# Weight pieces of four heads from each half of the heads, instead of eight heads in a row

## The chip, the cores and the metric

The kernel runs on one core of a Trainium2 chip. The time is device microseconds for one launch, from runs without the profiler. Three runs of the kernel before gave 1760.65, 1762.07 and 1762.35 us. Differences under 0.2% (3.5 us) can hardly be told from no change here.

## The reference, cut to what matters

Two blocks share an input of 2048 rows of 640 values. Block A is an attention whose memory is handed from segment to segment: 64 segments of 32 rows run one after the other, each with 8 memory rows that are the first 8 output rows of the segment before. Block B is a feed-forward block with a gate. The output mixes the two per row. All tensors are bfloat16.

```python
for s in range(n_seg):                      # 64 segments, in order
    xs = x[:, s*32:(s+1)*32, :]
    h = jnp.concatenate([mem, xs], axis=1)  # 8 + 32 rows
    q = jnp.einsum('btd,dhe->bhte', h, Wq)  # 32 heads of 192, Wq is 640 x 32 x 192
    k = jnp.einsum('btd,dhe->bhte', h, Wk)
    v = jnp.einsum('btd,dhe->bhte', h, Wv)
    p = softmax(mask(q k^T * 192**-0.5))
    o = jnp.einsum('bhte,hed->btd', p v, Wo)   # sum over all 32 heads
    mem = o[:, :8, :]                       # the next segment waits for this
    outs.append(o[:, 8:, :])
b = (gelu(x @ w_gate) * (x @ w_up)) @ w_down
return g * concat(outs) + (1 - g) * b       # g = sigmoid(sum(x * gate_w))
```

The heads don't meet before the sum in Wo, so it is free which heads are worked on together, as long as the rows of Wo match.

## The kernel before, in words

**Order of the whole.** Block B goes first (four blocks of 512 rows, up to about 160 us) while the weights of A are loaded. Then come the 64 segments, some 24.5 us each.

**Pieces of weights.** Wq, Wk and Wv are cut into 20 pieces each: piece `(m, o, k)` holds, for one group `o` of 8 heads (4 groups, 1536 columns) and one of 5 slices `k` of the model dimension, 128 partitions of 1536 values, 384 KB. Partition p of slice k is row 5p + k of the matrix, so that in HBM the rows of a piece stand 61,440 bytes apart, and each is one run of 3072 bytes (`piece_src`, L491 to L495). Wo is cut into 16 pieces `(3, p)`, one for each pair of heads, each one solid block of 480 KB, 3840 bytes to a partition.

**Swapped slots.** All 76 pieces don't fit into SBUF. 13 slots of Q, K and V pieces (3 Wq, 5 Wk, 5 Wv) are shared by head group 0 and head group 3, and 3 slots of Wo by pairs 0 to 2 and pairs 13 to 15 (`partner`, L545 to L549). Even segments go through the groups as 0, 1, 2, 3, odd ones as 3, 2, 1, 0. So in every segment the group that comes first is in place, each of its 13 + 3 slots is loaded anew as soon as TensorE has read it, and the new pieces are needed by the last group of the same segment; the next segment begins with that group. `swap_loads` (L612) puts these loads into the program behind the item that read the slot, and `load_piece` (L597) issues them, all on SyncE's queue (SP).

**Order within a segment.** The list `PROG` (L506) is the order of the work for TensorE: projections ("g", L1046 and, where the stationary operand is kept, L226), scores (L1087 to L1100), transposed probabilities (L1144, L1149), probabilities times V (L1177, L1179), the products with Wo of the first three groups (L1206), and those of the last group (L1229) as the segment's last work. `proj` takes the Q, K and V pieces by `piece`, `wo_part` those of Wo. VectorE then adds up the segment's output and transposes the 8 memory rows (L1371, L1375), and the next segment's first projection waits for that. Projections of the memory rows' outputs of other segments ("lf", L884) are spread over the list.

**Other work on SP's queue.** Between the weight loads SP issues, in program order, stores of pre-computed Q and K columns into a scratch (L895, L1276) and their loads (L935), the output stores (L956), the loads of x (L706) and of block B's result (L947). SP waits at each issue until the buffer is free, and the loads behind it in the queue wait with it. TensorE waits for a piece at the first matmul that reads it.

**At the start.** Before the segments, 40 pieces of Wq and Wk are issued in one row between 23 and 59 us (`load_residents`, L636, and `load_tmp`, L631), just ahead of the x load for the third block of B (L675).

Of the kernel before, what the change touches and what calls it, by code (L numbers as in the profile page):

```python
# [231 lines left out]
def _build(nc, A_x, A_mem0, A_Wq, A_Wk, A_Wv, A_Wo, seg_len, w_gate, w_up, w_down,  # L232
# [12 lines left out]
    NPAIR = NT // 2  # L245
    NOCT = NT // 4
# [13 lines left out]
    OW = 4 * 384  # L260
# [6 lines left out]
    S_ = _Sched(nc)  # L267
# [65 lines left out]
    o = wsA_base - wsB_total  # L333
# [6 lines left out]
    o = wsA_base  # L340
# [4 lines left out]
    o = ffn_base  # L345
# [4 lines left out]
    def bview(o, nbytes, plo=0, phi=128):  # L350
        return arena[plo:phi, o // 2:(o + nbytes) // 2]
# [4 lines left out]
    def sreg(o, nbytes, plo=0, phi=128):  # L356
        return Rg("sb", o, o + nbytes, plo, phi)
# [74 lines left out]
    o = ffn_base - sum(fp_sz.values())  # L432
# [50 lines left out]
    def psb(bank):  # L483
        return ps[:, bank, :].bitcast(BF)

    Wq2 = A_Wq.rearrange("d h e -> d (h e)").rearrange("(p k) n -> p k n", p=128)
    Wk2 = A_Wk.rearrange("d h e -> d (h e)").rearrange("(p k) n -> p k n", p=128)
    Wv2 = A_Wv.rearrange("d h e -> d (h e)").rearrange("(p k) n -> p k n", p=128)
    Wo2 = A_Wo.rearrange("h e n -> (h e) n").rearrange("(t p c) n -> p t c n", p=128, c=3)

    def piece_src(key):  # L491
        if key[0] == 3:
            return Wo2[:, key[1]]
        m, o_, k = key
        return (Wq2, Wk2, Wv2)[m][:, k, OW * o_:OW * (o_ + 1)]  # L495

    def piece_size(key):
        return GO if key[0] == 3 else GQ

    def piece_view(key, o):  # L500
        if key[0] == 3:
            return bview(o, GO).rearrange("p (c n) -> p c n", n=Dm)
        return bview(o, GQ)
# [16 lines left out]
    assert NOCT == 4  # L520
    WOP = 4
    NWP = NT
    NSW = 3
    NSQ = 13
    assert NWP == WOP * NOCT and 2 * NSW <= NWP

# [3 lines left out]
    def wo_pairs(s, item):  # L530
        lo, n = (WOP * item[1], WOP) if len(item) == 2 else (WOP * item[1] + 2 * item[2], 2)
        return [p if s % 2 == 0 else NWP - 1 - p for p in range(lo, lo + n)]
# [27 lines left out]
    tmp_off = {key: len(lk) * GQ + i * GQ for i, key in enumerate(lt)}  # L560
    assert (len(lk) + len(lt)) * GQ <= fp_base
    seq = lk + lv[2] + lw[NLW:] + lv[0] + lv[1] + lw[:NLW]
    res_off = {}
    o = 0
# [7 lines left out]
    r_res = {key: sreg(o, piece_size(key)) for key, o in res_off.items()}  # L572
# [23 lines left out]

    def load_piece(key, name):  # L597
        loaded[slot_id[key]] = key
        S_.add("sp", lambda e: e.dma_start(piece_view(key, res_off[key]), piece_src(key)), writes=[r_res[key]],
               dma_sem="slot%d" % slot_id[key], name="%s %s" % (name, key))  # L600

    def piece(seg, key):
# [9 lines left out]
    def swap_loads(seg, item):  # L612
        if item[0] == "g" and item[1] == 0 and 0 < item[2] < KT - 1:
            later.extend(key for key in done_keys if key[0] == 1)
            done_keys[:] = [key for key in done_keys if key[0] != 1]
        elif later:
            done_keys[:] = sorted(done_keys + later, key=lambda key: key[:1] + key[2:])
            del later[:]
        for key in done_keys:
            other = swap_in.get(key)  # L620
            if other is None or (other in partner) == (seg % 2 == 0):
                continue
            load_piece(other, "swap s%d" % seg)
        del done_keys[:]
# [5 lines left out]

    def load_tmp():  # L631
        for key in tmp_off:
            S_.add("sp", lambda e, key=key: e.dma_start(piece_view(key, tmp_off[key]), piece_src(key)),
                   writes=[r_tmp[key]], dma_sem="tmp%d" % (KT * key[0] + key[2]), name="tmp %s" % (key,))

    def load_residents(cls, pick=lambda key: True):  # L636
        for key in first:
            if slot_class[key] == cls and pick(key):
                load_piece(partner[key] if key in tmp_off else key, "res")
# [39 lines left out]
    for h in range(NH):  # L679
        for w_, sb_, rw_, nm in ((w_gate, wg_sb, r_wg, "wg"), (w_up, wu_sb, r_wu, "wu")):  # L680
            S_.add("sp", lambda e, h=h, w_=w_, sb_=sb_: e.dma_start(
                sb_[h], w_.rearrange("(p k) f -> p k f", p=128)[:, :, FH * h:FH * (h + 1)]),
                writes=[rw_[h]], dma_sem="%s%d" % (nm, h))
# [154 lines left out]
    x_stage(0)  # L838
    load_residents(0)
    load_tmp()  # L840
    for blk in range(NFB):
        if blk:
# [578 lines left out]
def bass_gated_mix__memory_aug_recurrent_mem_tr__glu_gated_geglu__prompt_kernel(  # L1421
    nc,
    A_x,
    A_mem0,
    A_Wq,
    A_Wk,
    A_Wv,
    A_Wo,
    A_seg_len,
    B_x,  # L1430
    B_w_gate,
    B_w_up,
    B_w_down,
    gate_w,
    out,
):
    _build(nc, A_x, A_mem0, A_Wq, A_Wk, A_Wv, A_Wo, A_seg_len, B_w_gate, B_w_up, B_w_down, gate_w, out)
# [33 lines left out]
```

## Time and profile before

| | |
|---|---|
| median of three runs | 1762.07 us (1760.65 to 1762.35) |
| span of the profiled execution | 1765.1 us |
| TensorE matmuls busy | 1623.9 us, 92% of the span |
| VectorE, ScalarE, GpSimd busy | 960.0, 802.8, 320.0 us |
| granted TensorE clock, mean | 0.994 |
| moved by DMA | 499.57 MB, mean 283 GB/s |
| share of the 16 DMA engines' time, SP's queue | 78.3% |
| weight loads in the profile | 335 Wk, 335 Wv, 209 Wq of 384 KB; 205 Wo of 480 KB |

In the profile PE is TensorE's matmuls, PEld its weight loads, DVE VectorE, ACT ScalarE, POOL GpSimd, SP SyncE; an engine's name with a q is its queue of waits and DMA issues. L599 is line 599 of the kernel. A group's "idle before" is the idle time of its engine ahead of it. A DMA's time "to landing" runs from its issue to the semaphore that tells of its last byte. The profiled execution is 3.0 us (0.17%) longer than the median without the profiler.

### The profile page before, as it was taken

Reading aid. Unit: us, or ns where it says so; the run is one execution under the profiler, and the core shown is the slowest. Engines: PE = TensorE matmul, PEld = TensorE weight load, DVE = VectorE, ACT = ScalarE, POOL = GpSimd, SP = SyncE. Lnnn points to the kernel's source line nnn. Section 1 sums busy time; section 2 is a strip of 40 time slices with the busy share of each in tenths; the row PEclk is TensorE's granted clock in tenths of the full one; section 3 lists DMA queues with packets and bytes.
Section 4 is the critical chain, followed back from the end, with each engine's and each line's share of the span. In section 5 each row is a group of like instructions: output and inputs, shape, how many; then the busy total and the mean of one; then the engine's idle time right before and its main releaser. Section 6 shows DMA issues by size and latency. Waiting matters only on the chain.

```text
span 1765.1 us, 80301 instructions
## 1 busy us (share of the span) xinstructions
PE 1623.9 (92%) x39162; PEld 809.5 (46%) x31501; DVE 960.0 (54%) x2932; ACT 802.8 (45%) x1835; POOL 320.0 (18%) x1099
## 2 busy tenths in 40 slices
PE   9999999999999999999999989999999998999887
PEld 4554444444444444454444444454444444454444
DVE  2222655556555655555555655555555655655554
ACT  3222544545444544444444544444444544445443
POOL 1100111111112112111212111111211121121211
PEclk9999999999999999999999999999999999999999
DMA  9814987888778887888788887879787886879776
GB/s 335 295 48 157 329 313 250 320 313 288 280 269 311 299 308 253 315 290 319 281 280 293 296 293 250 314 285 323 279 280 275 311 310 241 312 282 327 283 275 238
DMA packets 271311, 499.57 MB, mean 283 GB/s; under 512 B 105304, under 2 KB 132208, under 8 KB 270960
## 3 DMA queue, kind: packets, MB, share of 16 engines
q1 hardware_dynamic: 267832, 491.34, 78.3%
q8 instruction: 276, 4.52, 1.0%
q10 hardware_dynamic: 3128, 3.09, 0.6%
q14 instruction: 75, 0.61, 0.1%
HBM read 473.22 MB, written 21.11 MB: 280 GB/s over the span
## 4 chain that ended last, share of the span: by engine, by line
PE 71%; DVE 15%; DMA 6%; issue 4%; ACT 4%; DVEq 0%; SPq 0%; ACTq 0%
PE ps L1046 20%; PE ps L226 15%; PE ps L1206 8%; DMA arena<-in_A_Wo_dram 5%; PE ps L1177 3%; PE ps L804 3%; PE ps L801 3%; PE ps L884 3%; PE ps L1100 3%; PE ps L819 2%; PE ps L1087 2%; DVE ps L1114 2%; DVE arena L1112 2%; PE ps L1095 2%; PE ps L1229 2%
## 5 line engine op out<-in xcount | busy, mean ns | idle before, releaser
L1046 PE MATMUL ps<-arena 128*32 128x384 bf16 x9940 | 723.0, 329 | 42.4 <-DVE arena L1375 34.4
L226 PE MATMUL ps<-arena 128*32 128x384 bf16 x7680 | 595.4, 328 | 7.9 <-DVE arena L1215 3.5
L1046 PEld LDWEIGHTS ps<-arena 128*32 128x32 bf16 x9940 | 257.5, 97 | 365.3 <-issue 226.0
L1080 DVE STREAM_TRANSPOSE arena<-arena 128x384 bf16<-128x384 bf16 x512 | 270.8, 557 | 150.8 <-ACT arena L1066 149.2
L1066 ACT ACTIVATE arena<-ps 128x384 bf16<-128x384 f32 x512 | 236.2, 489 | 211.6 <-PE ps L1046 196.3
L1206 PE MATMUL ps<-arena 128*32 128x320 bf16 x6144 | 293.6, 301 | 13.9 <-issue 13.4
L1124 ACT ACTIVATE ps<-ps 104x160 f32<-104x160 f32 x256 | 71.9, 281 | 293.4 <-DVE ps L1114 293.4
L1206 PEld LDWEIGHTS ps<-arena 128*32 128x32 bf16 x6144 | 163.5, 97 | 74.0 <-issue 19.4
L1112 DVE TENSOR_REDUCE arena<-ps 104x4 f32<-104x160 f32 x256 | 83.0, 324 | 165.8 <-PE ps L1100 164.6
L941 POOL COPY arena<-arena 128x96 bf16<-128x96 bf16 x256 | 70.3, 275 | 513.4 <-PE ps L1100 444.2
L1188 ACT ACTIVATE arena<-ps 128x480 bf16<-128x480 f32 (+1 forms) x256 | 137.0, 535 | 43.8 <-PE ps L1179 39.6
L1196 POOL COPY arena<-arena 128x96 bf16<-128x96 bf16 x256 | 68.3, 267 | 441.1 <-ACT arena L1188 357.3
L1162 ACT ACTIVATE arena<-ps 128x448 bf16<-128x448 f32 x192 | 104.2, 543 | 96.7 <-PE ps L1149 96.4
L1069 ACT ACTIVATE arena<-ps 128x384 bf16<-128x384 f32 x256 | 125.1, 489 | 20.9 <-PE ps L1046 16.3
L1177 PE MATMUL ps<-arena 128*64 128x160 bf16 x1536 | 123.1, 243 | 12.5 <-ACT arena L1162 6.9
L1126 DVE TENSOR_REDUCE arena<-ps 104x4 f32<-104x160 f32 x256 | 83.0, 324 | 92.5 <-ACT ps L1124 92.5
L1177 PEld LDWEIGHTS ps<-arena 128*64 128x64 bf16 x1536 | 80.8, 109 | 91.6 <-issue 31.7
L884 PE MATMUL ps<-arena 128*32 128x384 bf16 x1280 | 111.4, 330 | 2.2 <-issue 2.0
L1179 PE MATMUL ps<-arena 128*64 128x64 bf16 x1536 | 104.8, 193 | 4.1 <-issue 4.1
L891 DVE STREAM_TRANSPOSE arena<-arena 128x384 bf16<-128x384 bf16 x128 | 73.7, 576 | 31.6 <-ACT arena L889 27.8
L1215 DVE TENSOR_TENSOR arena<-ps,arena 64x160 f32<-64x160 f32 x160 | 50.8, 317 | 72.3 <-ACT arena L1212 61.6
L1114 DVE TENSOR_TENSOR ps<-ps,arena 104x160 f32<-104x160 f32 x256 | 85.0, 332 | 8.8
(84 smaller groups left out, 1819.2 us busy)
## 6 DMA issues: line engine op xcount, KB each, us to landing
arena<-in_A_Wk_dram SPq DMA_DIRECT2D x335, 384.0 KB, 7.1
arena<-in_A_Wv_dram SPq DMA_DIRECT2D x335, 384.0 KB, 9.1
arena<-in_A_Wo_dram SPq DMA_DIRECT2D x205, 480.0 KB, 6.4
arena<-in_A_Wq_dram SPq DMA_DIRECT2D x209, 384.0 KB, 5.4
arena<-left_qk_scratch SPq DMA_DIRECT2D x126, 96.0 KB, 2.8
left_qk_scratch<-arena SPq DMA_DIRECT2D x49, 192.0 KB, 2.3
left_qk_scratch<-arena SPq DMA_DIRECT2D x30, 96.0 KB, 5.7
ffn_b_scratch<-arena ACTq DMA_DIRECT2D x16, 160.0 KB, 4.4
```

What stands on the lines that cost most here:

```text
L226: return e.add_instruction(mybir.InstMatmult(name=nm, start_tensor_calc=like["start"], stop_tensor_calc=stop, tile_size=(128, 32), tile_po ...
L884: fns.append(lambda e, outp=outp, rhs=rhs, j=j: e.matmul(outp, lhs, rhs, start=(k == 0), stop=(k == KT - 1), tile_position=(0, 32 * j)))
L1046: fns.append(lambda e, outp=outp, rhs=rhs, j=j: e.matmul(outp, lhs, rhs, start=(k == 0), stop=(k == KT - 1), tile_position=(0, 32 * j)))
L1066: S_.add("act", lambda e, m=m, bk=bk: e.activation(out=rows_sb[m], in_=ps[:, bk, 0:384], func=ACTF.Copy), reads=[r_ps[bk]], writes=[r_rows ...
L1069: S_.add("act", lambda e, i=i, bk=bk: e.activation(out=v_sb[i % NVB].rearrange("p (c n) -> p c n", c=3), in_=ps[:, bk, 0:384].rearrange("p ...
L1080: S_.add("dve", lambda e: e.transpose(out=dst[:, :, 0:L], in_=rows_sb[m].rearrange("p (c r) -> p c r", r=L)), reads=[r_rows[m]], writes=[r ...
L1112: S_.add("dve", lambda e: e.tensor_reduce(out=mxs, in_=S3, axis=AX.X, op=ALU.max), reads=[rb], writes=[rst], name="smax max")
L1114: S_.add("dve", lambda e: e.tensor_tensor(out=S3, in0=S3, in1=mxb, op=ALU.subtract), reads=[rb, rst], writes=[rb], name="smax sub")
L1177: return [lambda e: e.matmul(full, v[:, e0:e0 + 64], PTm[:, i], start=True, stop=False, tile_position=(0, 64 * i), skip_group_check=True), ...
L1179: lambda e: e.matmul(part, vl[:, e0:e0 + 64], PTl[:, i], start=False, stop=True, tile_position=(0, 64 * i), skip_group_check=True)]
L1188: S_.add("act", lambda e: e.activation(out=apx(u[:, 0, 0, :], [[R, na], [3 * R, 4], [1, R]]), in_=ps[:, A, 0:na * W].rearrange("p (c t r) ...
L1206: fns.append(lambda e, i=i, t=t, j=j, gv=gv: e.matmul(ps[32 * j:32 * j + 32, bank, 0:2 * DJ].rearrange("p (h n) -> p h n", h=2), lhs2[i], ...
```

## The change

A head group is no longer 8 heads in a row but 4 heads of the first sixteen and the 4 that stand at the same place among the second sixteen. A row of a Q, K or V piece is then two runs of 1536 bytes, 6144 bytes apart in HBM, where it was one run of 3072 bytes. Both runs go into the same place in SBUF, next to each other, in the same transfer. The pair of heads t of group o is pair 8 (t // 2) + 2 o + t % 2 of the matrix, and the Wo pieces are taken by that; each is still one solid block. The instructions of all engines, their order and the sizes of the tiles are the same; only the addresses from which SP's weight loads read are others.

```diff
+    WOP = 4
...
     def piece_src(key):
         if key[0] == 3:
-            return Wo2[:, key[1]]
+            o_, t = key[1] // WOP, key[1] % WOP
+            return Wo2[:, NPAIR * (t // 2) + 2 * o_ + t % 2]
         m, o_, k = key
-        return (Wq2, Wk2, Wv2)[m][:, k, OW * o_:OW * (o_ + 1)]
+        return (Wq2, Wk2, Wv2)[m][:, k].rearrange("p (h o n) -> p o h n", h=2, o=NOCT)[:, o_]
+
+    def piece_dst(key, o):
+        v = piece_view(key, o)
+        return v if key[0] == 3 else v.rearrange("p (h n) -> p h n", h=2)
...
-        S_.add("sp", lambda e: e.dma_start(piece_view(key, res_off[key]), piece_src(key)), writes=[r_res[key]],
+        S_.add("sp", lambda e: e.dma_start(piece_dst(key, res_off[key]), piece_src(key)), writes=[r_res[key]],
...
-            S_.add("sp", lambda e, key=key: e.dma_start(piece_view(key, tmp_off[key]), piece_src(key)),
+            S_.add("sp", lambda e, key=key: e.dma_start(piece_dst(key, tmp_off[key]), piece_src(key)),
```

More of the change, by code (lines that the diff above doesn't have):

```diff
@@ L520, in _build @@
     assert NOCT == 4
-    WOP = 4
     NWP = NT
```

## The prediction, made before the result was known

> **What bounds the kernel now.** I read the page first, then who waited for the weight loads, then one segment's issues and its chain, and last the speed of the DMA engines with rows of different lengths.
>
> The page:
>
> ```profile
> span 1765.1 us, 80301 instructions
> ...
> DMA packets 271311, 499.57 MB, mean 283 GB/s; under 512 B 105304, under 2 KB 132208, under 8 KB 270960
> ...
> q1 hardware_dynamic: 267832, 491.34, 78.3%
> ...
> PE 71%; DVE 15%; DMA 6%; issue 4%; ACT 4%; DVEq 0%; SPq 0%; ACTq 0%
> ```
>
> TensorE carries 71% of the chain that ended last, but 6% of it, some 106 us, goes through DMAs, and the page's list by line puts 5% on the loads of Wo. Queue q1, SP's, keeps the 16 DMA engines busy for 78.3% of the span. So the DMA engines are the second resource, and not far from the first. Of the packets, 270,960 - 132,208 = 138,752 lie between 2 and 8 KB: they are the 879 Q, K and V loads and the 205 Wo loads, at 128 rows each. A row is one packet.
>
> Who waited for the loads of L599, the weight loads in the segments (us in total, times):
>
> ```profile
>   PEld ps L1229: 8.6, 12
>   PE ps L1229: 6.1, 10
>   PEld ps L1046: 2.4, 6
> ```
>
> With 0.5 us on a fourth row this is 17.6 us in all: TensorE waits little for weights, and nearly always at L1229, the segment's last products with Wo.
>
> One segment (number 5), SP's issues by start and length:
>
> ```profile
> 305.12 0.50 SPq L599 DMA_DIRECT2D arena<-in_A_Wk_dram  x1
> 305.67 2.56 SPq L599 DMA_DIRECT2D arena<-in_A_Wq_dram  x3
> 308.27 2.80 SPq L599 DMA_DIRECT2D arena<-in_A_Wk_dram  x4
> 311.12 2.15 SPq L599 DMA_DIRECT2D arena<-in_A_Wv_dram  x4
> ...
> 314.48 1.58 SPq L599 DMA_DIRECT2D arena<-in_A_Wv_dram  x1
> 318.23 0.38 SPq L1276 DMA_DIRECT2D left_qk_scratch<-arena  x1
> 318.65 1.03 SPq L599 DMA_DIRECT2D arena<-in_A_Wo_dram  x2
> ...
> 320.20 0.55 SPq L599 DMA_DIRECT2D arena<-in_A_Wo_dram  x1
> ```
>
> and its end in the chain:
>
> ```profile
> 320.14 0.06 PE ps L1206
> 320.20 6.85 DMA arena<-in_A_Wo_dram
> 327.05 0.04 issue
> 327.10 0.42 PE ps L1229 x12
> ```
>
> 13 pieces go out within 11 us, and the engines take about 1.0 us for each, so a line forms: the last Wo piece stands 6.85 us in it, lands at 327.05, and the segment's last matmuls start 0.05 us later. What the 13 pieces ahead of it take longer, it lands later.
>
> The same for all segments: I set the landing of each of the 16 swapped pieces against the first matmul that waits for it, from the trace's issues, times to landing and matmuls, and took the smallest spare time of each of the 64 segments. It is at the end of the wait (0.04 us) in 21 segments, 0.1 to 0.6 us in 7, 0.6 to 1 us in 11, 1 to 2 us in 18 and more in 7. Of the segments whose number leaves 1 when divided by 4, which run the most extra work on SP, 15 of 16 have none to spare.
>
> The speed of the DMA engines when they are full: three stretches, 9 to 13 us (w_gate and w_up, 768 bytes a row), 17 to 20 us (w_down, 1280 bytes) and 314 to 319 us (the Q, K and V pieces, 3072 bytes):
>
> ```profile
> DMA packets 1969, 1.48 MB, mean 369 GB/s; under 512 B 48, under 2 KB 1969, under 8 KB 1969
> ...
> DMA packets 941, 1.19 MB, mean 396 GB/s; under 512 B 13, under 2 KB 941, under 8 KB 941
> ...
> DMA packets 737, 2.03 MB, mean 406 GB/s; under 512 B 81, under 2 KB 81, under 8 KB 736
> ```
>
> The reader sees that short rows cost speed, but not much. The rows under 512 B here are the 4-byte semaphore writes.
>
> **The change part by part.** (1) *Engines.* PE, DVE, ACT and POOL get the same instructions in the same order; cost 0, no cover needed. Wo: other blocks, equally solid, 3840 bytes a row; 0.
>
> (2) *Rows.* Each of the 879 Q, K and V loads becomes 256 rows of 1536 bytes instead of 128 of 3072: 112,512 packets more. What does one more packet cost? One engine spends 16 x 768 / 369 = 33.3 ns on 768 bytes, 16 x 1280 / 396 = 51.7 ns on 1280 and 16 x 3072 / 406 = 121.1 ns on 3072. The two short rows give 18.4 ns for 512 bytes and so 5.7 ns that come with any packet. From a line between 1280 and 3072 bytes, 1536 would take 61.6 ns, and two of them 2.1 ns more than one of 3072. The packets' own recorded times (median 36 ns for 768 bytes, 55 for 1280, 121 for 3072), which overlap a little, give 8 ns. So 2.1 to 8 ns, and I take 5.5, since 1536 lies next to the pair of short rows. An engine has 8 rows of each piece: 8 x 5.5 = 44 ns a piece (17 to 64), and 13 pieces put the Wo loads 0.57 us back (0.22 to 0.83).
>
> (3) *What of it TensorE feels.* In each segment I let the nth piece of Q, K or V land n x 44 ns later, Wo 13 x 44 ns, and took the largest amount by which a piece then misses its first matmul. 28 of 64 segments are late, by 12.5 us in sum: 8.6 us in the segments of remainder 1 (15 x 0.57), 2.8 in those of remainder 2, 1.1 in the rest. The next segment starts that much later, with its loads, so the delays add. At 17 ns a piece the sum is 4.4 us, at 33 ns 8.9, at 64 ns 20.5, at 80 ns 27.5. The remaining 36 segments hide the added 0.57 us behind their spare time; without that the sum would be 64 x 0.57 = 36 us.
>
> (4) *SP's issue.* An issue of a piece takes 0.43 us in the median; one of w_gate with 640 rows 0.62 to 0.92 us, a scratch store of 512 rows 0.38. So 0 to 0.2 us more for 256 rows; I take 0, because at 1.0 us a piece the engines stay behind SP either way. At the start SP is held once about 12 pieces are under way; if that limit counts rows, it will be 6. Then the last Wv issue (it lands at 322.73) ends near 317 instead of 316.06. Behind it stands the store that waits for DVE until 318.2; cover 1 us, and if it were gone, the line at the engines would still be 5 us long. The out store and the x load between the Wv loads are in the same line now. Cost 0.
>
> (5) *Who else waits in the line.* SP waits at L935 for a scratch store (72.5 us, 15 times) and at L947 for an output store (25.8 us, 26 times), and GpSimd's L973 and VectorE's L975 need L947's data. All land later by the same 0.57 us, and mostly in segments of remainder 1, where TensorE shifts as much; VectorE has 0.1 to 0.8 us to spare there before the next L1080. Between 0 and 0.57 us in 16 segments, 0 to 9 us; I take 0, since both sides shift together.
>
> (6) *The start.* The x load issued at 58.80 stands behind 40 pieces: 40 x 44 ns = 1.8 us. It lands at 72.39 and its transposes start at 75.27; hidden. At 80 ns it would cost 0.3 us.
>
> Sum: 1765.1 + 12.5 = 1777.6 us in the profile; the median lies 3.0 us under the profile, so 1774 us (+0.7%).
>
> **The rivals.** *No difference.* If the DMA engines move 1536-byte rows as fast as 3072-byte ones, the price per packet falls to the 2.1 ns or to nothing, and the sum to 4 us or less: 1762 to 1765.5. For it: 396 against 406 GB/s are 2.5% apart, and the longer stretch is disturbed by more semaphore writes. Against it: 369 GB/s at 768 bytes. The Trainium skill's page "DMA: Bandwidth & Descriptors" says under Specifications that transfers of 512 bytes and up run at line rate, the rule that speaks for this rival. The trace agrees only in part: 768 bytes reached 91% of the speed of 3072.
>
> *Faster.* The 3072-byte rows took 121 ns in the median but 132 in the mean; some 2,400 of them, 38 a segment, took over 300 ns, mostly as a stream starts. If two runs from places 6144 bytes apart do away with these, a row costs 11 - 5.5, about 6 ns, less, 0.6 us over 13 pieces. In the 21 segments that wait, about 0.5 us of it counts, since some waits are shorter: 10 us, 1752; with all waits gone 17.6 us, 1744. It decides once the saving passes 5.5 ns a row. Against it: 9 of 10 rows already are at the median, and the address pitch between rows is unchanged.
>
> *Much slower.* If such long packets come with each packet rather than with each byte, a row costs 11 + 5.5 = 17 ns more, 0.135 us a piece, 1.8 us at Wo. The sum of step 3 then lies between 36.6 us (0.1 us a piece) and 68.5 (0.155), about 56: 1818. Against it: 768-byte rows were 41 ns in the mean against 36, 1280-byte rows 58.5 against 55; the excess shrinks with the row.
>
> **How the numbers follow.** My forecast (4.5 to 28 us more, 1766.5 to 1790) has 0.66, no difference 0.15, faster 0.08, much slower 0.11. The bound of what can be told from no change is 0.2%, 3.5 us. Slower: 0.66 + 0.11, less 0.01 for a forecast that ends just inside the bound, 0.76; the same 0.16; faster 0.08. The range leaves out the faster case, most of the much slower one and the lower part of no difference: 1762 to 1795.
>
> **What the profile after would show.** Packets of SP's queue up by 112,512 to about 380,000, nearly all of the new ones under 2 KB. The stretch of full engines in a segment at 385 to 400 GB/s instead of 406. Waits at L1229 for the Wo loads up from 14.7 us to about 27, the L1046 waits by 1 or 2 us; DMA's share of the chain up from 6% to 10% or more; busy times of the engines unchanged. It is wrong if the packets don't double, if the speed at 1536 bytes leaves the 369 to 406 GB/s, if the waits grow at lines other than L1229 and L1046, or if SP is held where the Wo loads are issued.

## The result, and the profile after

The changed kernel takes 1791.32 us (median of four runs, 1784.64 to 1794.64), the kernel before beside it 1762.21 us: a ratio of 1.0172, 95% interval 1.0145 to 1.0199. The change costs 29 us, where 12 were forecast. The profiled executions are 25.4 us apart, 1790.5 against 1765.1 us, at granted clocks of 0.997 and 0.994, so the clock is not the cause.

The page of the kernel after (the fourth and fifth lines are DMA queues: packets, MB, share of 16 engines' time):

```profile
span 1790.5 us, 80301 instructions
PE 1627.9 (91%) x39162; PEld 810.0 (45%) x31501; DVE 962.0 (54%) x2932; ACT 802.3 (45%) x1835; POOL 320.3 (18%) x1099
DMA packets 383823, 499.57 MB, mean 279 GB/s; under 512 B 105304, under 2 KB 357232, under 8 KB 383472
q1 hardware_dynamic: 380344, 491.34, 80.5%
q8 instruction: 276, 4.52, 1.0%
PE 69%; DVE 14%; DMA 8%; issue 5%; ACT 4%; DVEq 0%; POOL 0%; ACTq 0%; SPq 0%; POOLq 0%
```

The packets have risen by exactly 112,512, all under 2 KB, and the instructions are the same. In the chain that ended last DMA went from 6% to 8%, and "issue", which the prediction did not look at, from 4% to 5%.

Who waited for the weight loads, now at L604 (the lines after it have moved by 5: L1234 was L1229, L1051 was L1046):

```profile
  PEld ps L1234: 13.8, 19
  PE ps L1234: 10.0, 18
  PEld ps L1051: 7.4, 16
  PE ps L1051: 2.0, 5
```

PEld and PE can stand in the same wait, the weight load into the array and the matmul behind it, so the rows must not be added up, as the prediction did with its 17.6 us. The matmuls alone waited 6.6 us in 12 places before and 12.0 us in 23 after. That is 5 us of the 25.

The rest is in rows that name no releaser. The view of waits, TensorE alone (line, what ended the wait: us in total, times, longest us), of the kernel before:

```profile
PE ps L1206 <- issue: 13.4, 14, 2.0
...
PE ps L1046 <- issue: 5.4, 8, 1.3
PE ps L1177 <- issue: 4.8, 6, 1.5
...
PE ps L1095 <- issue: 0.9, 2, 0.5
...
PE ps L1100 <- issue: 0.8, 2, 0.5
```

and of the kernel after:

```profile
PE ps L1211 <- issue: 14.7, 14, 1.8
...
PE ps L1051 <- issue: 9.7, 13, 1.6
...
PE ps L1182 <- issue: 6.2, 6, 1.5
PE ps L1105 <- issue: 4.5, 8, 1.4
...
PE ps L1100 <- issue: 4.2, 6, 1.0
```

All rows of this kind come to 33.9 us in 48 places before and 51.1 us in 71 after. I laid the idle stretches of matmuls and weight loads together, each stretch counted once: 132.9 us before and 153.9 us after, 21.1 us more (without the 1.4 us at the very start). Of that +17.1 us are "issue", +5.4 us waits for weights, -1.4 us all else. Outside idle stretches TensorE takes 4.2 us longer. Sum 25.3 of the 25.4 us.

What is TensorE waiting for, when no semaphore is late? The same instruction in both kernels, in the timeline of TensorE (start us, length, line, operation, count, idle before and its end). Before:

```profile
393.06 0.26 PE L1095 MATMUL ps<-arena 128*40 128x40 bf16 x7
393.73 0.20 PE L1095 MATMUL ps<-arena 128*40 128x40 bf16 x1 [0.41 <-issue]
```

After:

```profile
398.16 0.26 PE L1100 MATMUL ps<-arena 128*40 128x40 bf16 x7
399.35 0.20 PE L1100 MATMUL ps<-arena 128*40 128x40 bf16 x1 [0.93 <-issue]
```

Eight equal matmuls stand in the program in a row, with no wait between the seventh and the eighth, and yet the eighth starts late, in both kernels. About 2.5 us earlier a packet of another queue was under way; the DMA view of 391.2 to 391.4 us before,

```profile
q8 instruction: 1, 0.02, 33.7%
```

and of 396.6 to 396.8 us after:

```profile
q8 instruction: 1, 0.02, 34.9%
```

The trace gives their starts as 391.32 and 396.68 us, with 1.08 and 1.12 us for each. There are 276 such packets of 16,384 bytes in both kernels. PE and PEld together are 39,162 + 31,501 = 70,663 instructions, and 70,663 / 276 = 256.03. So one packet goes with every 256 instructions of TensorE, and I read it as TensorE's own code. All 44 idle stretches over 0.2 us without a releaser before, and all 66 after, end 2.2 to 2.7 us after the start of such a packet; a moment taken at random does so in about 8% of cases. I read the stretches as TensorE running out of code, because its next 256 instructions came late. That they came late because the packet stood in line with the weight loads is what the experiments have to show. The Trainium skill's page "Runtime: NRT & Kernel Launch" says under Instruction fetch mechanics that code is fetched in blocks of 16 KiB, 256 instructions, and that a crossing is "mostly hidden". The block agrees with the 256.03 here. The cover does not: 34 us are open before and 51 after.

### The profile page after: what moved, and what is told of

Same layout as the page of the kernel before. It is cut to its first block, busy times and chain, and to the rows that moved or that the text cites. A ratio compares the mean times of both kernels' runs of the same rounds, so it can differ in the third digit from the quotient of the medians.

```text
span 1790.5 us, 80301 instructions
## 1 busy us (share of the span) xinstructions
PE 1627.9 (91%) x39162; PEld 810.0 (45%) x31501; DVE 962.0 (54%) x2932; ACT 802.3 (45%) x1835; POOL 320.3 (18%) x1099
## 4 chain that ended last, share of the span: by engine, by line
PE 69%; DVE 14%; DMA 8%; issue 5%; ACT 4%; DVEq 0%; POOL 0%; ACTq 0%; SPq 0%; POOLq 0%
PE ps L1051 19%; PE ps L226 14%; PE ps L1211 7%; DMA arena<-in_A_Wo_dram 7%; PE ps L1182 3%; PE ps L809 3%; PE ps L806 3%; PE ps L1105 3%; PE ps L889 3%; PE ps L824 2%; DVE ps L1119 2%; PE ps L1092 2%; PE ps L1234 2%; DVE arena L1117 2%; PE ps L1100 2%
## 5 line engine op out<-in xcount | busy, mean ns | idle before, releaser
L1051 PE MATMUL ps<-arena 128*32 128x384 bf16 x9940 | 725.4, 329 | 48.1 <-DVE arena L1380 33.8
L1051 PEld LDWEIGHTS ps<-arena 128*32 128x32 bf16 x9940 | 258.5, 97 | 373.3 <-issue 229.5
L1211 PE MATMUL ps<-arena 128*32 128x320 bf16 x6144 | 294.0, 300 | 15.6 <-issue 14.7
L1182 PE MATMUL ps<-arena 128*64 128x160 bf16 x1536 | 123.6, 243 | 13.9 <-ACT arena L1167 6.2
L1234 PE MATMUL ps<-arena 128*32 128x160 bf16 x3072 | 75.0, 234 | 16.8 <-DMA arena<-in_A_Wo_dram 10.0
```

Of the source, the lines that this page charges most:

```text
L1051: fns.append(lambda e, outp=outp, rhs=rhs, j=j: e.matmul(outp, lhs, rhs, start=(k == 0), stop=(k == KT - 1), tile_position=(0, 32 * j)))
L1182: return [lambda e: e.matmul(full, v[:, e0:e0 + 64], PTm[:, i], start=True, stop=False, tile_position=(0, 64 * i), skip_group_check=True), ...
L1211: fns.append(lambda e, i=i, t=t, j=j, gv=gv: e.matmul(ps[32 * j:32 * j + 32, bank, 0:2 * DJ].rearrange("p (h n) -> p h n", h=2), lhs2[i], ...
L1234: S_.add("pe", [lambda e, j=j, c=c, g_=g_, p=p: e.matmul(ps[32 * j:32 * j + 32, OB2, SC:512], u[:, p % 4, c, 0:L], g_[:, c, DJ * j:DJ * (j ...
```

## The experiments

Three theories went into the runs. **A**, the prediction's mechanism with a larger price: rows take longer, the weights land later, TensorE waits for them. **B**: the code packets stand longer behind the weight loads, and TensorE waits for code. **C**: it is the 6144 bytes between the two runs, not their number. For each run I give the matmuls' idle time that ends in "issue" as *code* and the time that ends in a weight load as *weights*, summed from the view of waits. Before: code 33.9, weights 6.6; after: 51.1 and 12.0. Each ratio is to runs of the kernel before taken beside the run (medians 1759.8 to 1768.6 us).

**Runs 3072 bytes apart** (C). The group takes its two runs from one half of the columns:

```diff
-            return Wo2[:, NPAIR * (t // 2) + 2 * o_ + t % 2]
+            return Wo2[:, NPAIR * (o_ // 2) + 2 * (o_ % 2) + 4 * (t // 2) + t % 2]
-        return (Wq2, Wk2, Wv2)[m][:, k].rearrange("p (h o n) -> p o h n", h=2, o=NOCT)[:, o_]
+        half = (Wq2, Wk2, Wv2)[m][:, k, 2 * OW * (o_ // 2):2 * OW * (o_ // 2 + 1)]
+        return half.rearrange("p (h o n) -> p o h n", h=2, o=2)[:, o_ % 2]
```

> Two runs of 1536 bytes to a row as in the changed kernel, but 3072 bytes apart in HBM instead of 6144 (a group is four heads and the four that stand eight heads further on; the Wo pairs match). Theory A (each packet more costs its DMA engine a fixed time, so the weights land later and TensorE waits for them): as the changed kernel, ratio to before 1.013 to 1.021, median row 65 ns. Theory B (TensorE's own code comes over the same engines and comes later): the same ratio. Theory C (it is the place of the two runs in HBM that costs): another ratio, under 1.01 or over 1.03.

1793.97 us, ratio 1.0195 (1.0174 to 1.0217); code 53.3. It is like the changed kernel, so halving the distance changes nothing that can be told, and C falls.

**The order of Wo alone**, Q, K and V as before:

```diff
-            return Wo2[:, key[1]]
+            o_, t = key[1] // 4, key[1] % 4
+            return Wo2[:, NPAIR * (t // 2) + 2 * o_ + t % 2]
         m, o_, k = key
         return (Wq2, Wk2, Wv2)[m][:, k, OW * o_:OW * (o_ + 1)]
```

> The changed kernel's order of the Wo pieces alone, with the rows of Q, K and V of the kernel before (so each head's result meets another head's Wo rows). All theories: no difference, ratio 0.998 to 1.002. If it is over 1.005, the blocks of Wo are part of the cause.

1762.04 us, 1.0019 (1.0002 to 1.0036); code 34.3, weights 7.1. The other Wo blocks cost 0.2%, 0.36% at the most; nearly all of the cost is in the rows of Q, K and V.

**Four runs of 768 bytes**, three packets more to a row instead of one:

```diff
-            return Wo2[:, NPAIR * (t // 2) + 2 * o_ + t % 2]
+            return Wo2[:, WOP * t + o_]
-        return (Wq2, Wk2, Wv2)[m][:, k].rearrange("p (h o n) -> p o h n", h=2, o=NOCT)[:, o_]
+        return (Wq2, Wk2, Wv2)[m][:, k].rearrange("p (h o n) -> p o h n", h=4, o=NOCT)[:, o_]
...
-        return v if key[0] == 3 else v.rearrange("p (h n) -> p h n", h=2)
+        return v if key[0] == 3 else v.rearrange("p (h n) -> p h n", h=4)
```

> Four runs of 768 bytes to a row: a group is two heads of each quarter of the heads, Wo pairs to match. Theory A: four packets of 36 ns (median; 41 ns mean) against one of 121 (132): 23 to 32 ns more a row, 0.18 to 0.26 us a piece, 2.4 to 3.4 us at the last Wo load; by the table of spare times, 90 to 140 us more, ratio 1.05 to 1.08, nearly all of it waits of TensorE for weights. Theory B: the stretches in which TensorE waits for nothing but its code grew by 17 us for one packet more a row; three packets more make about 50 us, ratio 1.03, and most of it is such stretches.

1863.83 us, 1.0591 (1.0543 to 1.0640). Who waited for the weight loads of this kernel:

```profile
  PE ps L1051: 36.5, 61
  PE ps L1234: 32.2, 39
```

Weights 69.4, but code only 29.7. At this dose A has the size and B misses. A likely reason, not shown by this run, is that code can arrive while TensorE stands waiting for weights, so that the one wait covers the other. This run cannot tell what the 29 us of two runs are.

**No weight loads in the segments.** The swapped slots keep what they have, from the kernel before:

```diff
     def load_piece(key, name):
         loaded[slot_id[key]] = key
+        if name.startswith("swap"):
+            return
```

> The kernel before without the 16 weight loads of each segment (the shared slots keep what the first loads brought, so half of the groups multiply by another group's weights). Theory A: only TensorE's waits for weights go, 7 us by the union of matmuls and weight loads: 1750 to 1757 us. Theory B: the stretches in which TensorE waits for its code go as well, 34 us in the kernel before: 1715 to 1735 us, and these stretches fall under 10 us.

1702.17 us, 0.9678 (0.9655 to 0.9702). Its page:

```profile
span 1700.0 us, 79358 instructions
...
PE 1596.8 (94%) x39162; PEld 796.8 (47%) x31501; DVE 955.1 (56%) x2932; ACT 802.0 (47%) x1835; POOL 319.1 (19%) x1099
```

There is no "issue" row left for TensorE's matmuls, with the same 276 code packets: the code waits come from the weight traffic. The gain, 58 us, is more than either theory said. The 34 us of code and the 6.6 us of weights account for 40; between the two profiled executions, 65 us apart, busy PE is 27 us lower as well, for the same matmuls. The clock, 0.999 against 0.994, would account for some 8 us of these 27; the rest is not explained.

**Loads that nobody reads.** This is the run that tells A from B. The swapped loads go out as before, same rows, same moments, but into slots that no matmul reads, so that no matmul in the segments can wait for them. The slots are those of head group 1, which reads the weights of group 2 instead:

```diff
+        if name.startswith("swap"):
+            alt = (3, 3 + key[1] % (NWP - NSW)) if key[0] == 3 else spare[key[0], key[2]]
+            op = S_.add("sp", lambda e: e.dma_start(piece_view(alt, res_off[alt]), piece_src(key)), writes=[r_res[alt]],
+                        dma_sem="slot%d" % slot_id[alt], name="%s %s" % (name, key))
...
+            return
```

With one run in a row, as in the kernel before:

> The kernel before, with its 16 weight loads in each segment issued at the same places and after the same releases, but into slots that nobody reads (groups 1 take the weights of groups 2, Wo pairs 3 to 5 those of 6 to 8, and the shared slots keep what the first loads brought, so the result is another one). TensorE then never waits for a weight load in the segments. Theory A: 7 us less than before, 1750 to 1757 us. Theory B: the same here, with about 34 us left in which TensorE waits for its code.

With two runs, as in the changed kernel:

> The same edit on the changed kernel: the loads with two runs of 1536 bytes to a row, unread. Theory A: the late weights can't be felt, so the time is that of the same edit on the kernel before, within 0.3%. Theory B: 12 to 20 us above it, and the stretches in which TensorE waits for its code are 12 to 20 us longer.

One run: 1764.88 us, 1.0005 (0.9982 to 1.0028); code 30.1, weights 2.5. Both theories had 7 us less than before, and the median is no lower. Two runs: 1789.13 us, 1.0130 (1.0100 to 1.0160); code 53.9, weights 3.0. Two runs cost 24 us, more than the 12 to 20 that B said, although TensorE hardly waits for weights: A falls as the cause of most of the 29 us, and the code waits grow by 23.8 us. The two profiled executions are 31.9 us apart, as that with one run was among the fastest of its ten; 8.1 us of that are busy time of TensorE, and the code is nearly all of the rest. TensorE's longest code waits with one run,

```profile
PE ps L1224 <- issue: 8.4, 11, 1.2
```

and with two:

```profile
PE ps L1229 <- issue: 15.5, 14, 1.6
```

(It is the same line, L1206 of the kernel before; what was added above it has moved the number.) The few waits for weights left are from the loads ahead of the first segment.

**Two runs in V alone**, a smaller dose (335 of 879 loads, 38% of the new packets):

```diff
-            o_, t = key[1] // WOP, key[1] % WOP
-            return Wo2[:, NPAIR * (t // 2) + 2 * o_ + t % 2]
+            return Wo2[:, key[1]]
...
+        if m < 2:
+            return (Wq2, Wk2)[m][:, k, OW * o_:OW * (o_ + 1)]
...
-        return v if key[0] == 3 else v.rearrange("p (h n) -> p h n", h=2)
+        return v if key[0] != 2 else v.rearrange("p (h n) -> p h n", h=2)
```

> Two runs of 1536 bytes to a row for the V pieces alone, 5 of the 13 swapped pieces of a segment (V's heads then don't match those of Q and K, so the result is another one); Q, K and Wo as before. Theory B: five thirteenths of the 29 us, 8 to 15 us more, with the stretches without a releaser at 38 to 45 us. Theory A: by the table of spare times 5 pieces put the Wo loads 0.38 us back: 6 to 9 us more, all of it waits for weights.

1774.46 us, 1.0071 (1.0044 to 1.0099), 13.8 us more than before; code 47.1, weights 6.8. The code waits grew by 13.2 us, weights by 0.2. B's expectation of the time is met, with the stretches slightly longer than it said.

**Four runs that nobody reads**, to see whether the code waits go on growing when no wait for weights covers them:

> The unread loads (slots that nobody reads, as in the two kernels before of that kind) with four runs of 768 bytes to a row. Theory A: no wait for weights can count, 1750 to 1770 us. Theory B1 (the line that TensorE's code stands in is a given number of bytes on its engine, some 74 KB, and drains more slowly with short rows): it lasts some 24% longer than with one run, 3.6 us instead of 2.9, and the stretches without a releaser go from 30 to 80 us or more, the time to 1810 us or more. Theory B2 (the line is a given number of rows): 64 rows of 41 ns are 2.6 us, shorter than now, stretches 20 to 35 us, 1745 to 1765 us.

1823.64 us, 1.0351 (1.0320 to 1.0382); code 45.4, weights 3.1. The code waits do not grow beyond those of two runs. They are longer than the 29.7 of the four runs that are read, which bears out that waits for weights cover code waits there. Counted by the instruction that TensorE has reached, the packets start (median) 2.90 us after the earliest that any kernel shows, against 2.89 with one run nobody reads and 3.11 with two. Neither of the two sizes in the expectation holds; the time is in B1's range, but not for B1's reason. The two sizes compare lines of the same bytes or rows, and the line is neither: with four runs SP's issue of a weight load in the segments takes 0.87 us in the median instead of 0.42, and for hardly any time are more than six under way, against nine with one run. Part of the time comes from elsewhere. SP is held at its issues, and the store of Q and K columns (the store that was L1276) goes out late. ScalarE waits for its landing before it can write V (the copy that was L1069) into the buffer that the store reads, and TensorE waits for ScalarE: its waits for ScalarE are 35.6 us, against 13.9 with one run that nobody reads (matmuls and weight loads together).

**A shorter line.** If B holds, fewer loads under way must bring the code sooner. Load n of the swaps waits for load n - 6, n - 4 or n - 3:

```diff
+    swaps = []
...
+        if name.startswith("swap"):
+            swaps.append(op)
+            if len(swaps) > 4:
+                op.deps.add(swaps[-5])
```

> The kernel before, with at most 6 swapped pieces under way: SP issues a swap only when the sixth before it has landed (8 to 9 are under way now at the end of the V loads). Theory B (TensorE's code stands in the line behind the weight rows on its engine): with 6 pieces under way a code packet started some 2.8 us after its turn, as with 8, so little change: 1752 to 1764 us. Theory A (only late weights cost): no change, or slower by some us where SP is held.

> The kernel before with at most 4 swapped pieces under way. Theory B: with 4 under way a code packet started 2.1 us after its turn instead of 2.8, so that the 34 us of stretches without a releaser shrink to 8 to 20 us, and the time to 1738 to 1755 us, with the weight waits at 5 to 15 us. Theory A: the loads can only land later: 1762 to 1775 us, and the stretches stay at 34 us.

> The same with at most 3. A load takes 3.0 us at the least from issue to landing, 1.0 of it on the engines, so 3 just keep the engines full. Theory B: stretches without a releaser under 10 us (1.5 us late with 3 under way), weight waits up, in sum 1735 to 1765 us. Theory A: 1765 to 1800 us by later weights, stretches unchanged.

> The changed kernel with at most 4 swapped pieces under way. Theory B: most of the 17 us more of stretches without a releaser go, and most of the rest too: 1745 to 1768 us, 5 to 15 us above the same line with one run to a row. Theory A: 1791 us or more, 25 to 30 us above the same line with one run to a row.

| loads under way | median us | ratio (95%) | code | weights | clock |
|---|---|---|---|---|---|
| one run, 6 | 1759.24 | 0.9985 (0.9963 to 1.0007) | 22.8 | 12.7 | 0.992 |
| one run, 4 | 1834.73 | 1.0387 (1.0330 to 1.0445) | 2.5 | 77.1 | 0.982 |
| one run, 3 | 2012.14 | 1.1416 (1.1384 to 1.1448) | 0 | 198 | 0.945 |
| two runs, 4 | 1863.92 | 1.0567 (1.0512 to 1.0622) | 0.4 | 97.6 | 0.971 |

The code waits fall as B said, and further, from 33.9 to 22.8, 2.5 and 0. With six the time fits both theories. With one run and four or three it is far above what either said: the weights now arrive late, and take more than the code gives. With two runs and four it is 29 us above one run and four, as A said (25 to 30) and not B (5 to 15); 20.5 us of that are waits for weights. These runs alone do not part the two: a TensorE that waits for weights could be hiding its code waits, as with four runs. So the same limit went onto the loads that nobody reads.

> The unread loads, one run to a row, with at most 4 of them under way. They move the same bytes, and their lateness can't be felt. Theory B (the code stands in the line behind the weight rows): the stretches without a releaser fall from 30 to under 10 us, the time from 1765 to 1725 to 1745 us. Theory A, or any in which the load of the DMA engines as such costs: no change, 1755 to 1770 us.

> The same with two runs to a row. Theory B: the 24 us between one run and two runs go with the line: stretches under 10 us, and within 8 us of the same kernel with one run. Theory A: 1780 to 1795 us, as without the limit.

One run: 1784.71 us, 1.0091 (1.0068 to 1.0115), code 11.0, weights 2.7. Two runs: 1801.33 us, 1.0180 (1.0153 to 1.0208), code 12.1, weights 3.0. With hardly a wait for weights to hide behind, the code waits fall from 30.1 to 11.0 and from 53.9 to 12.1. Waits for other engines grew and could hide some of that, but the packets themselves are earlier too: by the same count they start 1.8 to 2.0 us after the earliest, instead of 2.9 and 3.1. The shorter line brings the code about 1 us sooner.

The time went up all the same, and two runs stayed 16.6 us behind one, so the expectation of the times was missed by both theories. What took the gain stands behind the loads in SP's queue, which the prediction's steps 4 and 5 had put at 0. SP is held at the limited loads, and what it issues behind them goes out late. With one run, TensorE waits at L1199 (L1177 before) for ScalarE's copy of V, L1091 (L1069 before),

```profile
PE ps L1199 <- ACT arena L1091: 23.4, 15, 2.5
```

and in 13 of these 15 places ScalarE had waited for the landing of the store of Q and K columns (L1276 before):

```profile
ACT arena L1091 <- DMA left_qk_scratch<-arena: 25.3, 14, 2.7
```

The store takes 5.4 us from issue to landing, and 5.7 without the limit. But without the limit SP stood ahead of it for 59.7 us in all until its data was ready, and with the limit for less than 10 us: SP comes to it late. Block B's result is the second such path. GpSimd waits for it,

```profile
POOL arena L994 <- DMA arena<-ffn_b_scratch: 165.4, 59, 4.8
```

and what GpSimd does next comes late to TensorE:

```profile
PE ps L1109 <- POOL arena L964: 12.1, 15, 1.5
```

Of the 18 us between the two profiles (1782.5 and 1800.5) the waits for ScalarE are some 5 and time without gaps 9, with the clock at 0.990 and 0.984.

**Loads spread over the segment.** Instead of a limit behind which SP waits, a swapped load is put into the program after every 24 matmuls, two at the most in one place, and waits for the matmul before it:

```diff
+        if name.startswith("swap"):
+            op.deps.add(S_.streams["pe"][-1])
...
+    def pump(key=None):
+        n = sum(len(op.fns) for op in S_.streams["pe"][pace[0]:])
+        pace[0] = len(S_.streams["pe"])
+        pace[1] = min(2, pace[1] + n / 24)
+        while queue and (pace[1] >= 1 or key in [q[0] for q in queue]):
+            pace[1] = max(0, pace[1] - 1)
+            load_piece(*queue.pop(0))
...
-            load_piece(other, "swap s%d" % seg)
+            queue.append((other, "swap s%d" % seg))
```

> The kernel before with its swaps spread out: a swap goes into the program when 24 more matmuls (about 1.0 us) stand ahead of it than ahead of the swap before, two at once at the most, and waits for the last of these matmuls. No waiting for landings. Theory B: fewer pieces under way, stretches without a releaser 10 to 25 us instead of 34; weight waits 5 to 25 us; in sum 1740 to 1765 us. Theory A: weights can only land later, 1762 to 1785 us.

> The same edit on the changed kernel. Theory B: stretches without a releaser 10 to 30 us instead of 51, weight waits 10 to 35 us, 1755 to 1785 us. Theory A: 1790 us or more.

One run: 1764.88 us beside 1768.61, 0.9976 (0.9959 to 0.9992); code 32.0, weights 9.6. Two runs: 1790.28 us, 1.0128 (1.0057 to 1.0200); code 45.3, weights 16.5. The line hardly got shorter (4.0 pieces under way in the mean instead of 4.6 with one run, still five to seven for almost half of the time), so the code waits hardly fell, and B's expectation of them is missed in both. The first is a quarter of a per cent faster than the kernel before, and of the kernels that leave nothing out the only one whose interval lies below 1; it is too little to tell why.

## Why the prediction was wrong

The sign was right, and the time lies in the range of 1762 to 1795, but by luck: the forecast of +12 us names a mechanism, late weights, that carries 5 us of the 25 between the profiles. The larger part is late code, which the prediction does not have. Step by step:

- **Step 1, engines "cost 0, no cover needed", failed.** The engines do get the same instructions, but TensorE's come by DMA, in line with the loads that the change makes longer. This step hides the largest term: +17.1 of the 25.4 us, and 23.8 of the 31.9 us between the profiles of the two kernels whose loads nobody reads. The "issue" that stood at 4% in the chain shown was not asked about.
- **Step 2, the price of a packet, was too small.** A row of 1536 bytes took 65 ns in the median (70.9 in the mean), two of them 130 (141.8), one of 3072 bytes 121 (132.4). That is 9.0 to 9.4 ns for the added packet, not 5.5, and above the upper bound of 8: 72 to 75 ns a piece instead of 44. The full stretch from 315 to 320 us after:

```profile
DMA packets 1316, 1.93 MB, mean 385 GB/s; under 512 B 76, under 2 KB 1314, under 8 KB 1314
```

  385 GB/s, at the edge of the 385 to 400 forecast; 314 to 319 us gives 389, 318 to 322 us gives 376.
- **Step 3, the table of spare times, was too large.** At 75 ns a piece it gives some 25 us, by interpolation between 20.5 and 27.5. That would meet the measured span, and would be believed, had the unread loads not shown 24 us with the waits for weights nearly gone. The waits for weights grew by 5.4 us. Added up as the prediction did, with some waits counted twice, they rose from 14.7 to 23.8 us at L1229 (27 foreseen) and from 2.9 to 9.4 at L1046 (1 or 2 more foreseen). A likely part of the reason, not shown by a run of its own: a TensorE held up by its code also needs each weight later.
- **Step 4, SP's issue at no cost, held.** The median issue of a Wk piece went from 436 to 471 ns, of a Wv piece from 473 to 533, within the 0 to 0.2 us. The most weight loads under way at once ahead of the segments fell from 14 to 10, so if a limit holds SP there, it does not simply count rows, which would have halved it.
- **Step 5, others in the line, held for this change.** GpSimd's waits for block B's result went from 44.0 to 53.4 us, and the idle time of TensorE outside code and weights fell by 1.4. The path is real all the same: block B's result and, more, the store of Q and K columns that step 4 gave a cover of 1 us made TensorE wait when SP was held further, with four unread runs and with the limited unread loads.
- **Step 6, the start, held.** The first matmul of L1046, the projections, starts at 177.3 us instead of 177.1.
- **The rivals.** "No difference" is out at 1.0172. "Faster" and "much slower" both rested on the long packets, 11 ns of mean above the median: at 1536 bytes it is 5.9 ns a packet, 11.8 for two. It went with the bytes, so it was neither saved nor doubled.
- **The marks.** Packets and busy times came as foreseen, DMA's share of the chain reached 8% and not 10%. One of the marks of failure was "if the waits grow at lines other than L1229 and L1046". It did its work: L1095 grew from 0.9 to 4.2 us, L1100 from 0.8 to 4.5 and L1177 from 4.8 to 6.2, all with "issue" as what ended the wait.

What stays open is how far two runs should delay the code. In the segments of the kernel before, a code packet starts (median) 0.8 us after the earliest with no weight load under way, 1.4 with three, 2.5 with four and 2.9 with six or more; after, 0.8, 1.5, 2.7 and 3.1. The medians over all packets of these two traces are about 2.4 and 2.5 us; they hold 39,162 matmuls where those of the unread loads hold 39,181, all 19 missing ahead of the segments, so the two sets of medians can't be set side by side. A line that drains 7% slower (141.8 against 132.4 ns) would turn 2.9 into 3.1 us, which fits the two runs. With four runs unread the line holds fewer loads, so the median of 2.90 us there neither fits nor refutes it. Some 0.1 to 0.2 us on 276 packets can move the time so much only because what passes TensorE's remaining code counts: the cover ended for 48 packets before and for 71 after. The 4.2 us that TensorE takes longer outside idle stretches are not explained either.

## What to carry to other kernels

An unchanged stream of instructions is not free: it comes by DMA like the data, and here it came later the more weight loads were under way, until TensorE ran dry of code. Ask for the waits that end in "issue" and for the packets of the instruction queue before putting an engine down at 0, above all for TensorE with tens of thousands of matmuls. When a sum of one mechanism meets the measured time, take its wait away, with the load left in place, before believing it.

## What the runs showed of the chip that was not expected

- Loads that nobody waits for still cost time: the weight traffic in the segments is worth 58 us of 1760 here (0.9678 without it), of which about 34 us are code and 7 us weights; the rest is not explained.
- Rows are priced by packet well above 512 bytes: 369 GB/s at 768 bytes, 396 at 1280, 376 to 389 at 1536 and 406 at 3072, the last two in stretches that other packets disturb.
- The kernels in which TensorE stands idle longest show the lowest granted clock: 0.999 with no weight loads in the segments, 0.987 with four runs, 0.971 with two runs and four loads under way, 0.945 with 198 us of waits for weights. It does not hold in the small: before has 0.994 and after, with 21 us more idle time, 0.997.
- There is little room between too many loads under way and too few: with at most six swapped pieces the time is the same within 0.4%, with four 3.9% longer and with three 14%.
